# A thresholded attention followed by a SwiGLU block: chunks of 256 tokens instead of 384, two rows of gate or value products per PSUM bank, and an own place for raw weights

## Chip, cores, metric

One core of a Trainium2 chip. Times are device microseconds (us) of one execution; a kernel is timed in several runs, medians are quoted. The rounds ran on different chips, each with the kernel before beside it, so across rounds the ratios to the kernel before are the safer comparison. A profile is one execution recorded by the hardware profiler.

## The reference

```python
# q, k, v: (8 batches, 8 heads, 576 tokens, 64); all fp32
scores = q @ k.T / 8
thresh = max(scores, -1) - 0.02
scores = where(scores >= thresh, scores, -1e9)
attn   = softmax(scores)                       # (+1e-9 in the divisor)
x      = (attn @ v) -> (8*576 tokens, 512)
g      = x @ w_gate                            # w_gate, w_val: 512 x 1536
h      = g * sigmoid(g) * (x @ w_val)
out    = h @ w_out                             # w_out: 1536 x 512
```

## The kernel before

The kernel interleaves two kinds of work. The attention goes in **segments** (a pair of heads), these in **slots** (a tile of 128 queries): segments 0 to 3 have two slots, 4 to 7 three, 8 on five. "Slot 6.1" is slot 1 of segment 6. In each slot the scores, their maximum, the threshold, the exponential and the transposes go through VectorE (DVE), ScalarE (ACT) and GpSimd (POOL), while TensorE (PE) is kept full with **pieces** of the SwiGLU block of an earlier batch: a piece is the gate or value products of a row of 128 hidden units for one chunk of tokens, or three of the twelve accumulating output products (`po`). A slot's share of pieces is its **credit**: what is ready to be done, spread over the slots to come.

The weights arrive as raw 64-bit words in 24 parts. Each part is *fetched* (DMA), *split* on ACT, and *joined* by four DVE and two POOL instructions. A slot joins one. Where a piece asks for a weight that is not there yet, `need` forces further joins in a row, at that place in the program.

```python
    TC = 384                                     # tokens in a chunk
    # raw weights lie in parts of wo not yet filled, and in two buffers of xT
    places += [xp.tile([P, NCC, TC // (2 * G), 2, G], F32, name="xT")... for _ in range(2)]
    # ... (cut)
    def join_weights():
        # ... (cut)
        nc.vector.tensor_scalar(out=up, in0=up, scalar1=1.875 * 2.0 ** -64, ...)             # L169
        nc.vector.tensor_scalar(out=ub, in0=ub, scalar1=3, scalar2=0x7FFFFFFF, ...)          # L171
        nc.vector.scalar_tensor_tensor(out=ub, in0=hi, scalar=0x80000000, in1=ub, ...)       # L173
        nc.vector.tensor_scalar(out=ex.bitcast(U32), in0=ub, scalar1=0xFF800000, ...)        # L175
        nc.gpsimd.tensor_tensor(out=lo, in0=lo, in1=ex, op=ALU.mult)                         # L177
        nc.gpsimd.tensor_tensor(out=up, in0=up, in1=lo, op=ALU.add)                          # L178

    def need(n):                                 # force joins until n parts are there
        while len(joined) < n:
            fetch_weights(2)
            if not split: split_weights()
            join_weights()
            split_weights()

    def gate(j, cs, f, hts, gts):                # value() is alike, its eviction is a multiply on DVE
        # ... (cut)
        need(NCC * (f * P // TC + 1))
        for c in range(NCC):                     # one row: 4 matmuls
            nc.tensor.matmul(ps[:, 0:n], wgv[:, 0, c, f * P:(f + 1) * P], x[:, c, cs], ...)
        nc.scalar.copy(gts[f // per][:, f % per, :], ps[:, 0:n])

    def output(j, rows, hts):
        # ... (cut)
                if f % OF == 0:
                    if any(u[0] == j for u in unsig): sigmoids()
                    need(NCC * DFF // TC + DM // ne * (f * P // TC + 1))
                nc.tensor.matmul(po, hts[f // 2][:, f % 2, i * P:(i + 1) * P], wo[:, f, :], ...)

    # which token ranges are units of work of their own
        if j == 0:   waiting.extend([(0, 0, QA), (0, QA, TC)])        # QA = 256
        elif j == 1: waiting.extend([(1, 0, S - TC), (1, S - TC, TC)])
        else:        waiting.append((j, 0, TC))

    # one slot
            if n or x:
                fetch_weights(2)
                split_weights()
            # ... (cut)
            if more: join_weights()
            fill(part)                           # as many pieces as the credit allows
```

Segments 4 to 7 get the first SwiGLU work: the first 256 tokens of batch 0 are complete then. With chunks of 384 these 256 tokens are a part of chunk 0, whose output products (`wo`, the last weights to arrive) can't be called for before segment 9.

Of the kernel before, what the change touches and what calls it, by code (L numbers as in the profile page):

```python
# [18 lines left out]
def kernel(  # L19
# [42 lines left out]
    TC = 384  # L62
# [5 lines left out]
    assert 2 * D == P and NCC == NP and D == 2 * G and S - SM == 2 * G and 2 * S % TC == 0  # L68
# [6 lines left out]
    xp = ctx.enter_context(tc.tile_pool(name="xp", bufs=4))  # L75
    hp = ctx.enter_context(tc.tile_pool(name="hp", bufs=8))
    gp = ctx.enter_context(tc.tile_pool(name="gp", bufs=4))
    cv = ctx.enter_context(tc.tile_pool(name="cv", bufs=2))
# [19 lines left out]
    for x in sums:  # L98
# [7 lines left out]


# [8 lines left out]
    TW = 2 * TC  # L116
# [3 lines left out]
    places += [xp.tile([P, NCC, TC // (2 * G), 2, G], F32, name="xT").rearrange("p c t a r -> p (c t a r)")  # L120
               for _ in range(2)]
    for f in range(0, DFF, TC):
        for c in range(NCC):
            wpieces.append((wgv[:, :, c, f:f + TC], [w[c * P:(c + 1) * P, f:f + TC] for w in (w_gate, w_val)],
                            len(wpieces) % 4))
    nf, ne = TC // P, TW * P // TC
# [24 lines left out]
    def split_weights():  # L151
        if fetched:
            dst, place = fetched.popleft()
            words = places[place].rearrange("p (m n w) -> p m n w", m=dst.shape[1], w=2)
            lo = cv.tile([P, TW], F32, name="lo").rearrange("p (m n) -> p m n", m=dst.shape[1])
# [266 lines left out]

    unsig = []

    def rows_per(n):

        return 2 * (TC // n)

    def gate(j, cs, f, hts, gts):
# [7 lines left out]
        need(NCC * (f * P // TC + 1))  # L437
        ps = ps_f.tile([P, 512], F32, name="pg", tag="psf")
        x = xts[j].rearrange("p c t a r -> p c (t a r)")
        for c in range(NCC):  # L440
            nc.tensor.matmul(ps[:, 0:n], wgv[:, 0, c, f * P:(f + 1) * P], x[:, c, cs], start=(c == 0), stop=(c == NCC - 1))  # L441
        nc.scalar.copy(gts[f // per][:, f % per, :], ps[:, 0:n])  # L442

    def value(j, cs, f, hts, gts):
        n = cs.stop - cs.start
        per = rows_per(n)
        ps = ps_f.tile([P, 512], F32, name="pv", tag="psf")
        x = xts[j].rearrange("p c t a r -> p c (t a r)")
        for c in range(NCC):
            nc.tensor.matmul(ps[:, 0:n], wgv[:, 1, c, f * P:(f + 1) * P], x[:, c, cs], start=(c == 0), stop=(c == NCC - 1))  # L450
        nc.vector.tensor_tensor(out=hts[f // 2][:, f % 2, cs], in0=gts[f // per][:, f % per, :], in1=ps[:, 0:n],  # L451
                                op=ALU.mult)
        if f % per == per - 1:
            unsig.append((j, gts.pop(f // per), [hts[x][:, :, cs] for x in range((f + 1 - per) // 2, f // 2 + 1)]))
        if f == NF - 1 and cs.stop == TC:
            del xts[j]
# [11 lines left out]
    def output(j, rows, hts):  # L468
        for i in rows:
            po = ps_f.tile([P, 512], F32, name="po", tag="psf")[:, 0:DM]  # L470
            for f in range(NF):
                if f % OF == 0:
                    if any(u[0] == j for u in unsig):
                        sigmoids()
                    need(NCC * DFF // TC + DM // ne * (f * P // TC + 1))
# [16 lines left out]
    for j in range(NCHUNK):  # L492
        if j == 0:
            waiting.extend([(0, 0, QA), (0, QA, TC)])
        elif j == 1:
            waiting.extend([(1, 0, S - TC), (1, S - TC, TC)])
        else:
            waiting.append((j, 0, TC))

    def rows_of(unit):  # L500
        j, lo, hi = unit
        return range(lo // P if j else 0, hi // P if j or hi == TC else 0)
# [13 lines left out]
    def block():  # L516
        late = iter(())
        while True:
# [9 lines left out]
            c = HCOST * (hi - lo) / TC  # L528
            for f in range(NF):
# [22 lines left out]
    def start_batch(b):  # L552
        for j in range(b * S // TC, ((b + 1) * S - 1) // TC + 1):
            if j not in xts:
                while j - 4 in xts:
                    fill(HCOST)
# [82 lines left out]
    for n, seg in enumerate(segs):  # L639
        if NP <= n < 2 * NP:  # L640
            seg["v"] = segs[seg["i"]]["v"]
        for x, t in enumerate(seg["tiles"]):
# [11 lines left out]
            if attends and n > 2 * NP:  # L654
                if prev["i"] % NP == 0:
                    need(NCC * DFF // TC + DM // ne * DFF // TC)
# [4 lines left out]
            if n or x:  # L661
                fetch_weights(2)
                split_weights()
# [16 lines left out]
            if x == len(seg["tiles"]) - 2 and n + 1 < len(segs):  # L680
                prepare(segs[n + 1])
                fetch_qk(segs[n + 1]["i"] + 1)
# [40 lines left out]
```

## Time and profile before

| | before |
|---|---|
| time, median (range) of 3 runs | 1612.72 us (1612.72 to 1615.19) |
| PE busy | 1545.7 us, 96% |
| segments 4 to 7 / segment 8 / segments 9 to 11 | 94.5 / 61.3 / 120.1 us |
| segment 12 starts | 338.2 us |
| segments 12 to 19 / 20 to 34 / 35 to the end | 335.4 / 682.9 / 256.9 us |

Start and length of segments are read off the trace (first score matmul of each). PE is the bound once it is full, from 320 us on. What is to be had lies mostly before that.

### The profile page before, as it was taken

How to read it: one execution, taken by the hardware profiler on the slowest of the kernel's cores; microseconds unless marked ns; L12 is line 12 of the kernel's file. 1: busy time of each engine (PE TensorE's matmuls, PEld its weight loads, DVE VectorE, ACT ScalarE, POOL GpSimd, SP SyncE). 2: the span in 40 equal slices, each digit the busy share in tenths (PEclk: the TensorE clock that was granted, in tenths of full speed). 3: DMA queues.
4: the chain of work that ended last, by engine and by line, in shares of the span. 5: the costliest groups of instructions: out<-in, count | busy, mean ns of one | idle time of the engine just before them, and what ended most of it. 6: DMA issues, size and time to landing. Idle time of an engine off the chain costs nothing.

```text
span 1613.3 us, 28084 instructions
## 1 busy us (share of the span) xinstructions
PE 1545.7 (96%) x10384; PEld 854.9 (53%) x10384; DVE 1082.8 (67%) x3672; ACT 581.2 (36%) x1308; POOL 773.6 (48%) x692
## 2 busy tenths in 40 slices
PE   6899669999999999999999999999999999999998
PEld 4576555558555455455545545455545545455453
DVE  6888868878778778777767768677767767501000
ACT  5777623333333333333323424323323424312011
POOL 3546356554655646646545555636445554402011
PEclk9999889999999999999999999999999999999999
DMA  7442121111111211111011111111011120000000
GB/s 170 131 152 77 56 50 37 44 37 31 31 43 30 50 31 30 43 37 31 7 44 31 30 50 30 43 37 20 13 43 37 30 50 16 8 13 0 13 7 20
DMA packets 176344, 66.70 MB, mean 41 GB/s; under 512 B 159568, under 2 KB 159568, under 8 KB 176208
## 3 DMA queue, kind: packets, MB, share of 16 engines
q1 hardware_dynamic: 173328, 55.47, 15.2%
q0 software_dynamic: 2880, 9.44, 1.5%
q8 instruction: 82, 1.34, 0.3%
q14 instruction: 54, 0.44, 0.1%
HBM read 55.44 MB, written 9.44 MB: 40 GB/s over the span
## 4 chain that ended last, share of the span: by engine, by line
PE 81%; DVE 11%; issue 3%; ACT 3%; POOL 1%; DMA 1%; SPq 1%; DVEq 0%; POOLq 0%; ACTq 0%
PE pg L441 21%; PE pv L450 20%; PE po L476 20%; PE sc L255 9%; PE xa L390 8%; DVE p L295 3%; DVE mx L275 2%; DVE p L321 1%; PE sc L260 1%; ACT p L291 1%; DVE mx L232 1%; PE tp L339 1%; PE xa L362 1%; ACT L291 1%; POOL p L307 1%
## 5 line engine op out<-in xcount | busy, mean ns | idle before, releaser
L307 POOL TENSOR_SCALAR p<-p,ri 128x288 f32<-128x288 f32 x486 | 480.2, 1004 | 432.5 <-DVE ri L303 428.8
L441 PE MATMUL pg<-xT,wgv 128*128 128x384 f32 (+3 forms) x1344 | 410.0, 449 | 15.4 <-ACT gt L442 14.5
L450 PE MATMUL pv<-xT,wgv 128*128 128x384 f32 (+3 forms) x1344 | 407.8, 447 | 9.1 <-ACT gt L442 5.4
L476 PE MATMUL po<-wo,ht 128*128 128x512 f32 x864 | 387.8, 601 | 4.4 <-POOL ht L462 4.4
L441 PEld LDWEIGHTS pg<-xT,wgv 128*128 128x128 f32 x1344 | 243.3, 193 | 162.7 <-issue 24.5
L450 PEld LDWEIGHTS pv<-xT,wgv 128*128 128x128 f32 x1344 | 242.9, 192 | 150.4 <-issue 11.9
L295 DVE SCALAR_TENSOR_TENSOR p<-sc,th,p 128x288 f32<-128x288 f32 (+1 forms) x540 | 258.3, 529 | 47.3 <-ACT p L291 46.5
L476 PEld LDWEIGHTS po<-wo,ht 128*128 128x128 f32 x864 | 160.1, 190 | 210.3 <-issue 194.9
L287 ACT ACTIVATE th<-nm,cut 128x4 f32<-128x4 f32 (+1 forms) x140 | 41.6, 297 | 564.1 <-DVE nm L278 564.1
L275 DVE TENSOR_REDUCE mx<-sc 128x2 f32<-128x576 f32 x252 | 179.6, 750 | 94.7 <-PE sc L255 94.7
L291 ACT ACTIVATE p<-sc,nm 128x288 f32<-128x288 f32 (+1 forms) x540 | 237.1, 511 | 0.6
L451 DVE TENSOR_TENSOR ht<-gt,pv 128x384 f32<-128x384 f32 (+3 forms) x168 | 79.7, 485 | 176.1 <-PE pv L450 170.4
L255 PE MATMUL sc<-kT,qT 64*32 64x288 f32 x4032 | 170.9, 419 | 12.7 <-DVE p L295 12.7
L321 DVE STREAM_TRANSPOSE p<-p 128x576 f32<-128x576 f32 x252 | 181.3, 754 | 0.8 <-POOL p L307 0.8
L462 POOL TENSOR_TENSOR ht<-ht,gt 128x768 f32<-128x768 f32 (+3 forms) x84 | 130.3, 1582 | 95.1 <-ACT gt L460 95.1
L442 ACT COPY gt<-pg 128x384 f32<-128x384 f32 (+3 forms) x168 | 72.5, 439 | 179.1 <-PE pg L441 179.0
L390 PE MATMUL xa<-p,vall 64*64 64x288 f32 x2016 | 129.6, 405 | 0.4 <-issue 0.4
L255 PEld LDWEIGHTS sc<-kT,qT 64*32 64x32 f32 x4032 | 66.6, 107 | 118.1 <-issue 85.9
L390 PEld LDWEIGHTS xa<-p,vall 64*64 64x64 f32 x2016 | 78.2, 133 | 54.2 <-issue 15.4
L207 POOL TENSOR_SCALAR qraw<-qraw,scl 128x576 f32<-128x576 f32 x32 | 55.7, 1742 | 75.8 <-DMA qraw<-in_q_dram 51.8
L232 DVE TENSOR_REDUCE sums<-sums 32x4 f32<-32x4 f32 (+1 forms) x560 | 83.9, 150 | 10.5
L232 DVE TENSOR_REDUCE mx<-mx 32x4 f32<-32x4 f32 (+1 forms) x560 | 83.1, 148 | 10.4
(73 smaller groups left out, 854.4 us busy)
## 6 DMA issues: line engine op xcount, KB each, us to landing
vall<-in_v_dram SPq DMA_DIRECT2D x112, 144.0 KB, 3.5
qraw<-in_q_dram SPq DMA_DIRECT2D x128, 72.0 KB, 2.4
kraw<-in_k_dram SPq DMA_DIRECT2D x128, 72.0 KB, 2.8
out_dram<-ob POOLq DMA_DIRECT2D x36, 256.0 KB, 2.4
wo<-in_moe_w_gate_dram SPq DMA_DIRECT2D x16, 384.0 KB, 3.4
wo<-in_moe_w_val_dram SPq DMA_DIRECT2D x16, 384.0 KB, 4.0
xT<-in_moe_w_out_dram SPq DMA_DIRECT2D x6, 768.0 KB, 5.7
wo<-in_moe_w_out_dram SPq DMA_DIRECT2D x2, 768.0 KB, 4.4
```

The lines of the kernel that those rows point to most:

```text
L232: nc.vector.tensor_reduce(out=x[g * G:(g + 1) * G, 0:m, 1], in_=x[o * G:(o + 1) * G, 0:m, 0:1], axis=AX.X, op=ALU.max)
L255: nc.tensor.matmul(ps[g * G:(g + 1) * G, u, 0:SH], qT[hs, col + a * G:col + (a + 1) * G], kT[hs, c * SH:(c + 1) * SH], start=True, stop=True)
L275: nc.vector.tensor_reduce(out=mx[:, 2 * x:2 * x + 2, 0], in_=tile_[:, :, 0:SH], axis=AX.X, op=ALU.max, negate=True)
L291: nc.scalar.activation(ps[x], scs[x], AF.Exp, bias=nm[:, x:x + 1])
L295: nc.vector.scalar_tensor_tensor(out=ps[x], in0=scs[x], scalar=th[:, x:x + 1], in1=ps[x], op0=ALU.is_ge, op1=ALU.mult, accum_out=sm[:, x, ...
L307: nc.gpsimd.tensor_scalar(out=ps[x], in0=ps[x], scalar1=ri[:, x:x + 1], scalar2=None, op0=ALU.mult)
L321: nc.vector.transpose(out=p, in_=p)
L390: nc.tensor.matmul(xa[a][h * D:(h + 1) * D, at:at + n * G].rearrange("d (i q) -> d i q", q=G), vr[rs, h, j, :], p[rs, lo:lo + n, j, :], st ...
L441: nc.tensor.matmul(ps[:, 0:n], wgv[:, 0, c, f * P:(f + 1) * P], x[:, c, cs], start=(c == 0), stop=(c == NCC - 1))
L450: nc.tensor.matmul(ps[:, 0:n], wgv[:, 1, c, f * P:(f + 1) * P], x[:, c, cs], start=(c == 0), stop=(c == NCC - 1))
L462: nc.gpsimd.tensor_tensor(out=ht, in0=ht, in1=gt[:, 2 * x:2 * x + 2, :], op=ALU.mult)
L476: nc.tensor.matmul(po, hts[f // 2][:, f % 2, i * P:(i + 1) * P], wo[:, f, :], start=(f == 0), stop=(f == NF - 1))
```

## The change

Intent: one chunk of 256 fills half a PSUM bank, so two rows share a bank and an eviction takes both (114 evictions for each matrix instead of 168); the first 256 tokens are a whole chunk; raw weights get a place of their own and are loaded a slot ahead of their split, so that no split waits for a load.

```diff
-    TC = 384
+    TC = 256
+    FW = 384                                   # width of a part of the weights, as before
+    spare = const.tile([P, 6 * TW], F32, name="spare")
-    places += [xp.tile(... name="xT") ... for _ in range(2)]
+    places += [spare[:, n * 2 * TW:(n + 1) * 2 * TW] for n in range(2)]
+    los = deque(spare[:, n * TW:(n + 1) * TW] for n in (4, 5))
 ... (cut)
+    GR = 2
+    def rows_of_products(j, cs, f, mat, name):  # 2 rows, 8 matmuls, one bank
+        for i in range(GR):
+            for c in range(NCC):
+                nc.tensor.matmul(ps[:, i], wgv[:, mat, c, (f + i) * P:(f + i + 1) * P], x[:, c, cs], ...)
-        need(NCC * (f * P // TC + 1))
+        need(NCC * ((f + GR - 1) * P // FW + 1))
 ... (cut)
+        ends = [lo for lo in (QA - j * TC, S - j * TC) if 0 < lo < TC]     # cuts chunk 2 at 64
+        waiting.extend((j, lo, hi) for lo, hi in zip([0, *ends], [*ends, TC]))
-        return range(lo // P if j else 0, hi // P if j or hi == TC else 0)
+        return range(TC // P if hi == TC else 0)
 ... (cut)
-                    need(NCC * DFF // TC + DM // ne * DFF // TC)    # all weights, at segment 9
             if n or x:
+                split_weights()
                 fetch_weights(2)
-                split_weights()
+            if x == 0 and n >= NP:
+                fetch_qk(seg["i"] + 1)          # q and k at a segment's start, no longer at its end
```

The parts cut here also give the transposed tokens (`xT`) six buffers for four and the gates (`gt`) five for four.

More of the change, by code (lines that the diff above doesn't have):

```diff
@@ L61 @@
     SH = S // 2
-    TC = 384
+    TC = 256
+    XB = 6
     NCHUNK = B * S // TC
@@ L67 @@
     SCALE = 1.0 / float(D) ** 0.5
-    assert 2 * D == P and NCC == NP and D == 2 * G and S - SM == 2 * G and 2 * S % TC == 0
+    assert 2 * D == P and NCC == NP and D == 2 * G and S - SM == 2 * G and B * S % TC == 0
     const = ctx.enter_context(tc.tile_pool(name="const", bufs=1))
@@ L74 @@
     stp = ctx.enter_context(tc.tile_pool(name="stp", bufs=4))
-    xp = ctx.enter_context(tc.tile_pool(name="xp", bufs=4))
+    xp = ctx.enter_context(tc.tile_pool(name="xp", bufs=XB))
     hp = ctx.enter_context(tc.tile_pool(name="hp", bufs=8))
-    gp = ctx.enter_context(tc.tile_pool(name="gp", bufs=4))
-    cv = ctx.enter_context(tc.tile_pool(name="cv", bufs=2))
+    gp = ctx.enter_context(tc.tile_pool(name="gp", bufs=5))
     op = ctx.enter_context(tc.tile_pool(name="op", bufs=1))
@@ L105 @@
     wo = const.tile([P, NF, DM], F32, name="wo")
-    TW = 2 * TC
+    FW = 384
+    TW = 2 * FW
+    spare = const.tile([P, 6 * TW], F32, name="spare")
     wpieces = deque()
@@ L119 @@
     places = [land[:, n * 2 * TW:(n + 1) * 2 * TW] for n in range(NF * DM // (2 * TW))]
-    places += [xp.tile([P, NCC, TC // (2 * G), 2, G], F32, name="xT").rearrange("p c t a r -> p (c t a r)")
-               for _ in range(2)]
-    for f in range(0, DFF, TC):
+    places += [spare[:, n * 2 * TW:(n + 1) * 2 * TW] for n in range(2)]
+    los = deque(spare[:, n * TW:(n + 1) * TW] for n in (4, 5))
+    for f in range(0, DFF, FW):
         for c in range(NCC):
-            wpieces.append((wgv[:, :, c, f:f + TC], [w[c * P:(c + 1) * P, f:f + TC] for w in (w_gate, w_val)],
+            wpieces.append((wgv[:, :, c, f:f + FW], [w[c * P:(c + 1) * P, f:f + FW] for w in (w_gate, w_val)],
                             len(wpieces) % 4))
-    nf, ne = TC // P, TW * P // TC
+    nf, ne = FW // P, TW * P // FW
     wplaces = deque([4, 5, 2, 3] + [4, 5] * 2)
@@ L154, in split_weights @@
             words = places[place].rearrange("p (m n w) -> p m n w", m=dst.shape[1], w=2)
-            lo = cv.tile([P, TW], F32, name="lo").rearrange("p (m n) -> p m n", m=dst.shape[1])
+            lo = los[0].rearrange("p (m n) -> p m n", m=dst.shape[1])
+            los.rotate(1)
             nc.scalar.activation(dst, words[:, :, :, 1], AF.Abs, scale=2.0 ** -80)
@@ L425, in rows_per @@
     def rows_per(n):
-        return 2 * (TC // n)
+        return 2 if n > P else 4
+    GR = 2
+    def rows_of_products(j, cs, f, mat, name):
+        n = cs.stop - cs.start
+        ps = ps_f.tile([P, 512], F32, name=name, tag="psf")[:, 0:GR * n].rearrange("p (f n) -> p f n", n=n)
+        x = xts[j].rearrange("p c t a r -> p c (t a r)")
+        for i in range(GR):
+            for c in range(NCC):
+                nc.tensor.matmul(ps[:, i], wgv[:, mat, c, (f + i) * P:(f + i + 1) * P], x[:, c, cs],
+                                 start=(c == 0), stop=(c == NCC - 1))
+        return ps
     def gate(j, cs, f, hts, gts):
@@ L436, in gate @@
             gts[f // per] = gt[:, 0:per * n].rearrange("p (f n) -> p f n", n=n)
-        need(NCC * (f * P // TC + 1))
-        ps = ps_f.tile([P, 512], F32, name="pg", tag="psf")
-        x = xts[j].rearrange("p c t a r -> p c (t a r)")
-        for c in range(NCC):
-            nc.tensor.matmul(ps[:, 0:n], wgv[:, 0, c, f * P:(f + 1) * P], x[:, c, cs], start=(c == 0), stop=(c == NCC - 1))
-        nc.scalar.copy(gts[f // per][:, f % per, :], ps[:, 0:n])
+        need(NCC * ((f + GR - 1) * P // FW + 1))
+        ps = rows_of_products(j, cs, f, 0, "pg")
+        nc.scalar.copy(gts[f // per][:, f % per:f % per + GR, :], ps)
     def value(j, cs, f, hts, gts):
@@ L446, in value @@
         per = rows_per(n)
-        ps = ps_f.tile([P, 512], F32, name="pv", tag="psf")
-        x = xts[j].rearrange("p c t a r -> p c (t a r)")
-        for c in range(NCC):
-            nc.tensor.matmul(ps[:, 0:n], wgv[:, 1, c, f * P:(f + 1) * P], x[:, c, cs], start=(c == 0), stop=(c == NCC - 1))
-        nc.vector.tensor_tensor(out=hts[f // 2][:, f % 2, cs], in0=gts[f // per][:, f % per, :], in1=ps[:, 0:n],
+        ps = rows_of_products(j, cs, f, 1, "pv")
+        nc.vector.tensor_tensor(out=hts[f // 2][:, :, cs], in0=gts[f // per][:, f % per:f % per + GR, :], in1=ps,
                                 op=ALU.mult)
-        if f % per == per - 1:
-            unsig.append((j, gts.pop(f // per), [hts[x][:, :, cs] for x in range((f + 1 - per) // 2, f // 2 + 1)]))
-        if f == NF - 1 and cs.stop == TC:
+        if f % per == per - GR:
+            unsig.append((j, gts.pop(f // per), [hts[x][:, :, cs] for x in range((f + GR - per) // 2, f // 2 + 1)]))
+        if f == NF - GR and cs.stop == TC:
             del xts[j]
@@ L474, in output @@
                         sigmoids()
-                    need(NCC * DFF // TC + DM // ne * (f * P // TC + 1))
+                    need(NCC * DFF // FW + DM // ne * (f * P // FW + 1))
                 nc.tensor.matmul(po, hts[f // 2][:, f % 2, i * P:(i + 1) * P], wo[:, f, :],
@@ L492 @@
     for j in range(NCHUNK):
-        if j == 0:
-            waiting.extend([(0, 0, QA), (0, QA, TC)])
-        elif j == 1:
-            waiting.extend([(1, 0, S - TC), (1, S - TC, TC)])
-        else:
-            waiting.append((j, 0, TC))
+        ends = [lo for lo in (QA - j * TC, S - j * TC) if 0 < lo < TC]
+        waiting.extend((j, lo, hi) for lo, hi in zip([0, *ends], [*ends, TC]))
     def rows_of(unit):
         j, lo, hi = unit
-        return range(lo // P if j else 0, hi // P if j or hi == TC else 0)
+        return range(TC // P if hi == TC else 0)
     def cost(unit):
@@ L527, in block @@
             hts, gts = hidden.setdefault(j, {}), {}
-            c = HCOST * (hi - lo) / TC
-            for f in range(NF):
+            c = GR * HCOST * (hi - lo) / TC
+            for f in range(0, NF, GR):
                 if f == (EARLY if j else 0):
@@ L554, in start_batch @@
             if j not in xts:
-                while j - 4 in xts:
+                while j - XB in xts:
                     fill(HCOST)
@@ L681 @@
                 prepare(segs[n + 1])
-                fetch_qk(segs[n + 1]["i"] + 1)
+                if n < NP:
+                    fetch_qk(segs[n + 1]["i"] + 1)
         prev = seg
```

## The prediction

> **What bounds the kernel now.** I read the page first (parts 1, 2, 4), then the chain in order of time, then a table by stretches, then the timelines of the stretches where the matmul engine (PE) idles.
>
> ```profile
> span 1613.3 us, 28084 instructions
> PE 1545.7 (96%) x10384; PEld 854.9 (53%) x10384; DVE 1082.8 (67%) x3672; ACT 581.2 (36%) x1308; POOL 773.6 (48%) x692
> PE   6899669999999999999999999999999999999998
> DVE  6888868878778778777767768677767767501000
> PEclk9999889999999999999999999999999999999999
> ...
> PE 81%; DVE 11%; issue 3%; ACT 3%; POOL 1%; DMA 1%; SPq 1%; DVEq 0%; POOLq 0%; ACTq 0%
> ```
>
> PE is full from slice 8 on (40 us a slice): its idle time, 1613 - 1546 = 67 us, and its slow clock lie almost all in the first 320 us. Is a full PE at its best rate? The chain shows groups of eight gate or value records; each fp32 matmul leaves two records.
>
> ```profile
> 89.32 1.73 PE pv L450 x8
> 234.20 1.30 PE pv L450 x8
> 419.29 2.58 PE pv L450 x8
> ```
>
> These are widths 256, 192 and 384: 216, 162 and 322 ns a record, 0.84 ns a column in all three. So from slice 8 on only less PE work would help. The early part, with cuts at starts of scores:
>
> ```profile
> core 0: us, PE busy (x) PEld busy (x) DVE busy (x) ACT busy (x) POOL busy (x), PEclk, DMA share, GB/s
> 72.17:156.76 84.59, 82.80 (x579) 59.60 (x577) 71.56 (x151) 64.85 (x123) 44.24 (x26) 1.00 0.32 99
> 156.76:218.03 61.27, 38.71 (x354) 29.70 (x353) 49.73 (x143) 31.77 (x69) 28.36 (x17) 0.79 0.34 85
> 218.03:261.05 43.02, 39.12 (x355) 27.04 (x355) 34.02 (x117) 15.26 (x38) 20.01 (x19) 0.94 0.04 8
> 261.05:298.18 37.13, 35.36 (x272) 16.93 (x271) 31.61 (x118) 11.35 (x32) 26.11 (x29) 1.00 0.20 47
> ```
>
> The kernel runs in segments (a pair of heads each; 0 to 3 of two slots, 4 to 7 of three, 8 on of five). Segments 4 to 7 (62 to 157 us) have PE full. Segment 8 takes 61 us and has PE idle for 22; segment 9 takes 43; segment 10, with no weight work left, 37 at 85% DVE: that is the DVE-bound floor. In segments 8 and 9 the weights' joins (four DVE, two POOL operations a piece) are in the way, and one stall:
>
> ```profile
> 208.26 0.56 SPq L145 DMA_DIRECT2D xT<-in_moe_w_out_dram  x1
> 214.13 0.90 ACT L156 ACTIVATE wo<-xT 128x768 f32<-128x768 f32 x1 [7.97 <-DMA xT<-in_moe_w_out_dram]
> 216.02 2.08 PE L441 MATMUL pg<-xT,wgv 128*128 128x128 f32 x8 [9.42 <-ACT gt L442]
> ```
>
> The last weight load is issued in the slot that splits it, behind eight q/k loads that wait for DVE; ACT waits 8 us for it, PE 9.4 us for ACT. This the change removes.
>
> **What the Trainium skill says.** "TensorE: Matmul & The Clock Gate", section "Back-to-back issue gap", gives an isolated gap of N / 2.4 + 2.5 ns. The trace agrees with a pass of 2N columns per record: 384 gives 322.5, measured 322. So narrower chunks cost about 2.5 ns a record, little. The same page, section "Part 1: The HAM clock gate", says idle PE falls back to half clock; the trace has 0.79 in 157 to 218 us. "ScalarE: Activation LUTs", section "What ACT_TABLE_LOAD costs", gives about 1283 ns a load plus a drain; the trace has 1283 for each of 44. "PSUM — Partial Sum Buffer", section "The four PSUM rules": an output fits one bank of 512 fp32, so two rows of 256 fill one; the trace can't test it beyond the 512-wide output products.
>
> **The change, part by part.**
> (a) PE work. Gate and value have 1344 records each: 960 of 384 columns, 192 of 192, 96 of 256, 96 of 128. After: 19 units of 48 matmuls, 1824 records each: 1632 of 256, 96 of 192, 96 of 64. Old: 960 x 0.3225 + 192 x 0.1625 + 96 x 0.216 + 96 x 0.11 = 372 us. New: 1632 x 0.216 + 96 x 0.1625 + 96 x 0.08 (my estimate) = 376 us. Both matrices: +8 us, of which some +4 fall in the PE-bound part.
> (b) Evictions. 168 copies (72.5 us on ACT) become 114. By slope over the widths 256 and 384 (413, 541 ns on DVE), 512 takes about 670 ns on DVE; a 512 copy on ACT has 590 already. DVE saves some 6 us, ACT 8; in segments 8 to 11, DVE-bound, perhaps 5.
> (c) Sigmoids. They run once three units of two rows wait. Such units are a third smaller, so table pairs rise from 22 to about 33: +28 us on ACT, at 36% busy, hidden.
> (d) Loads. Splitting before fetching, own places, and q/k loads at a segment's start take away the 8 us stall and, in part, POOL's 52 us of waits on q. The latter lie beside a full PE: nothing.
> (e) Order of FFN work, the part that the few words do not name. I counted by hand from the code's credit rule which pieces fall in which slot. Chunk 0 is now complete with 256 tokens, so its output products belong to segments 4 to 8, and the pace rises. Before: 21 pieces of 1.73 us in segments 4 to 7, 36 us; after: 12 pieces of 3.45 and 3 output pieces of 2.57, 49 us. PE is full there: +13 us. The weights are wanted earlier, too: a pair of rows asks for the column block of its second row, and output weights are asked for at segment 7 instead of 9. Joins still go one a slot, else they are forced in a row. What one takes:
>
> ```profile
> 76.20 1.25 PE L260 MATMUL sc<-p 64*128 64x288 f32 x8
> ...
> 81.17 0.54 DVE L169 TENSOR_SCALAR wgv<-wgv 128x768 f32<-128x768 f32 x1
> ...
> 83.40 0.56 DVE L175 TENSOR_SCALAR wo<-wgv 128x768 uint32<-128x768 uint32 x1
> ...
> 84.09 1.82 POOL L177 TENSOR_TENSOR lo<-lo,wo 128x768 f32<-128x768 f32 x1 [3.08 <-ACT p L309]
> ...
> 86.00 1.82 POOL L178 TENSOR_TENSOR wgv<-wgv,lo 128x768 f32<-128x768 f32 x1
> ```
>
> The slot starts at 76.2, DVE joins at +5 to +7.8, POOL ends at +11.6. PE reaches its product at +3 to +5. Each further join in the slot adds about 3.7 us on POOL. Slots that now need a piece joined in the same slot, by my count: 4.1 (piece 7: wait about 5.5 us), 5.2 (piece 11: 5.7), 6.1 (pieces 13 to 15 in a row: POOL ends near +19, wait about 14), 7.2 (pieces 19 to 21: about 11), and 8.0 (22 and 23: the slot takes about 20). PE is in order, so the next scores stand behind the product and DVE idles meanwhile.
> Sum: segments 4 to 7 took 94.5 us; +13 work +36 waits, less some 6 already idle there: about 137. Segment 8: 20 + 26 (four slots at the floor) = 46 for 61. Segments 9 to 11: 37 each, 111 for 120. Net 43 - 15 - 9 = +19; less (b) 5 = +14; plus (a) 4 = +18; less about 4 for small waits that go (a tail with a smaller last chunk, q waits). About +13: 1612.7 + 13 = 1626 us.
>
> **The rivals.**
> R1, gain: the early stall goes, forced joins hide. DVE and POOL are at 85% and 52% in 72 to 157 us, so joins could overlap with pieces PE still has. Then segments 4 to 7 cost only the 13 us of work and segments 8 to 11 win 24: 1613 - 24 + 13 - 5 + 4 = about 1600. For it: the only join wait on PE before is 0.3 us. Against it: PE is in order and the product that waits is next in its queue.
> R2, nothing: PE is full at its best rate from 350 us on, all work moved is the same work, gains and losses early cancel: 1610 to 1617.
> R3, a new wait in the steady part: pieces of 3.45 us instead of 2.58 are coarser, and sigmoids forced just before an output product make PE wait for POOL (4.4 us in 3 times before). If each of some 30 rounds cost 1 us: 1645 to 1655. Against it: my count gives two forced rounds, for three before; slots with two pieces now hold 6.9 us, better matched to the DVE chain of 6.5 us a slot.
>
> **Range and chances.** My sum stands on waits estimated by hand; half of them gone gives 1608, R1 1600; all of them plus a cold clock after each (a restart record group took 2.08 instead of 1.06 us) gives some 1645. 8 in 10: 1600 to 1648. Faster by 2% (under 1580.5) would need 32 of the early idle us back with nothing paid: 0.05. Slower by 2% (over 1645): 0.12. Within 2%: 0.83.
>
> **What would show it.** Right: eight gate records of 256 in 1.73 us; segments 4 to 7 longer than 94.5 us with PE waits of 5 to 15 us on POOL's join in slots 6.1, 7.2, 8.0; no wait on the last weight load; segments 9 to 11 near 37 us; table loads near 66; the distance from segment 12 to the end the same within 6 us. Wrong: no PE waits on joins (then R1), or a steady part that is longer (R3), or a record of 256 that takes more than 0.22 us once streams are long.

## The result, and the profile after

| | before | after |
|---|---|---|
| time, median (range) | 1613.91 us (1612.72 to 1615.19) | 1702.55 us (1701.63 to 1704.14) |
| ratio, 95% interval | | 1.055 (1.0532 to 1.0568), slower |
| segments 4 to 7 | 94.5 us | 161.9 us |
| segment 8 | 61.3 | 54.1 |
| segments 9 to 11 | 120.1 | 121.2 |
| segment 12 starts | 338.2 | 398.7 (+60.5) |
| segments 12 to 19 | 335.4 | 351.8 (+16.4) |
| segments 20 to 34 | 682.9 | 683.2 (+0.3) |
| 35 to the end | 256.9 | 266.2 (+9.3) |

First the page of the kernel after, parts 1, 2 and 4 (40 slices of 42.5 us):

```profile
span 1699.9 us, 30018 instructions
PE 1569.8 (92%) x11344; PEld 1040.5 (61%) x11344; DVE 1094.6 (64%) x3642; ACT 603.0 (35%) x1315; POOL 797.0 (47%) x740
...
PE   6876648889999999999999999999999999899998
...
PEclk9987869899999999999999999999999999999999
...
PE 73%; DVE 9%; issue 3%; POOL 3%; ACT 2%; POOLq 0%; DVEq 0%; ACTq 0%
```

Counted from 0, PE was at 9 tenths in slices 2 and 3 before, and at 6 in the two after them; now it is at 4 to 7 from slice 2 to slice 5, and its clock falls to 6 tenths in slice 5. In the chain POOL has 3% for 1%. The table by stretches shows the same for segments 4 to 7 and segment 8 (columns as in the prediction's table). Segments 4 to 7 before:

```profile
62.26:156.76 94.50, 91.07 (x637) 65.26 (x637) 76.77 (x162) 73.24 (x139) 49.12 (x29) 0.98 0.34 105
```

Segments 4 to 7 and segment 8 after (segment 8 before is in the prediction):

```profile
61.50:223.40 161.90, 114.01 (x678) 76.37 (x679) 102.90 (x176) 85.25 (x148) 71.28 (x41) 0.84 0.26 81
223.40:277.50 54.10, 32.08 (x256) 16.90 (x255) 35.30 (x108) 12.25 (x30) 26.73 (x23) 0.81 0.11 27
```

In segments 4 to 7 of the kernel after no engine is full: PE 70%, DVE 64%, POOL 44%. The engines wait for one another, one after the other. The waits of PE name the place. Kernel before (engine, line, waited for: total us, times, longest):

```profile
PE pg L441 <- ACT gt L442: 14.5, 2, 9.4
PE sc L255 <- DVE p L295: 12.7, 20, 1.9
```

Kernel after:

```profile
PE po L485 <- POOL wo L181: 38.7, 4, 19.8
PE sc L258 <- DVE p L298: 29.1, 29, 3.9
PE pg L440 <- POOL wgv L181: 27.6, 5, 8.2
...
PE xa L393 <- DVE p L324: 6.0, 1, 6.0
```

PE's stall of 9.4 us is gone. In its place PE waits 66.3 us for the last instruction of forced joins (L181), nine times: 46.4 us of it in segments 4 to 7 and 19.8 in slot 8.0. It waits 16.4 us more than before for the scores' buffers (L298), nearly all from segment 9 on. ACT's own wait on a weight load, which the change was to remove, is still there, before and after:

```profile
ACT wo L156 <- DMA xT<-in_moe_w_out_dram: 8.0, 1, 8.0
ACT wo L159 <- DMA spare<-in_moe_w_out_dram: 7.4, 1, 7.4
```

In slot 7.2 two loads are issued at 210.36 us, and the first of them is split at 214.77. PE does not wait for this split: at that time it waits for an earlier join. The timeline of slot 6.1 shows a row of joins (start, duration, in brackets the idle time before it and its releaser). The first two lines are the lone join of slot 6.0, for comparison:

```profile
138.04 0.56 DVE L174 TENSOR_SCALAR wgv<-wgv 128x768 uint32<-128x768 uint32 x1
138.64 0.96 DVE L176 SCALAR_TENSOR_TENSOR wgv<-wo,wgv 128x768 uint32<-128x768 uint32 x1
...
147.47 1.99 POOL L180 TENSOR_TENSOR spare<-spare,wo 128x768 f32<-128x768 f32 x1 [3.36 <-ACT wgv L159]
147.84 2.04 DVE L174 TENSOR_SCALAR wgv<-wgv 128x768 uint32<-128x768 uint32 x1
149.54 2.00 POOL L181 TENSOR_TENSOR wgv<-wgv,spare 128x768 f32<-128x768 f32 x1
149.91 2.44 DVE L176 SCALAR_TENSOR_TENSOR wgv<-wo,wgv 128x768 uint32<-128x768 uint32 x1
151.57 0.91 ACT L160 ACTIVATE spare<-wo 128x768 f32<-128x768 uint32 x1 [4.65 <-POOL wgv L181]
...
151.59 1.22 PE L440 MATMUL pg<-xT,wgv 128*128 128x256 f32 x2 [5.64 <-POOL wgv L181]
...
157.26 1.22 PE L440 MATMUL pg<-xT,wgv 128*128 128x256 f32 x2 [4.45 <-POOL wgv L181]
...
162.50 1.22 PE L440 MATMUL pg<-xT,wgv 128*128 128x256 f32 x2 [4.02 <-POOL wgv L181]
```

A lone join has its two middle DVE instructions in 0.56 and 0.96 us. In the row they take 2.04 and 2.44 us, because they run beside POOL's two instructions of the join before (e6 tests this). Each starts while one of these runs and ends 0.42 and 0.81 us after the end of that one (149.46 and 151.54). Further joins therefore end 5.7 and 5.2 us apart (PE's starts at 151.59, 157.26 and 162.50), and not 3.7 us; in slot 7.2 5.8 and 5.7 us, and in slot 8.0, where POOL also has 4.64 us of p's normalisation (L310) to do between two joins, 8.3 us. ACT's half of a split also waits for POOL to free its buffer (4.65 us). Each further join releases one matmul (two records) of the second row of the pair, and PE stands again.

Where streams are long, the records have the predicted rate: within a group they start 216 ns apart. 16 records of 256 columns, two rows, take from start to start 480.13 - 476.58 = 3.55 us with the change of work, 222 ns each:

```profile
476.58 3.62 PE L440 MATMUL pg<-xT,wgv 128*128 128x256 f32 x16
```

### The profile page after: what moved, and what is told of

It is laid out like the page before. It is cut to its first block, busy times and chain, and to the rows that moved or that the text cites. A ratio compares the mean times of both kernels' runs of the same rounds, so it can differ in the third digit from the quotient of the medians.

```text
span 1699.9 us, 30018 instructions
## 1 busy us (share of the span) xinstructions
PE 1569.8 (92%) x11344; PEld 1040.5 (61%) x11344; DVE 1094.6 (64%) x3642; ACT 603.0 (35%) x1315; POOL 797.0 (47%) x740
## 4 chain that ended last, share of the span: by engine, by line
PE 73%; DVE 9%; issue 3%; POOL 3%; ACT 2%; POOLq 0%; DVEq 0%; ACTq 0%
PE po L485 19%; PE pg L440 19%; PE pv L440 19%; PE sc L258 8%; PE xa L393 8%; DVE p L298 2%; DVE mx L278 2%; POOL p L310 2%; DVE p L324 1%; DVE mx L235 1%; ACT L294 1%; ACT p L294 1%; POOL ht L471 1%; DVE sums L235 0%; POOL wo L181 0%
## 5 line engine op out<-in xcount | busy, mean ns | idle before, releaser
L310 POOL TENSOR_SCALAR p<-p,ri 128x288 f32<-128x288 f32 x504 | 498.0, 1004 | 515.0 <-DVE ri L306 513.1
L440 PE MATMUL pg<-xT,wgv 128*128 128x256 f32 (+2 forms) x1824 | 408.1, 377 | 27.6 <-POOL wgv L181 27.6
L440 PE MATMUL pv<-xT,wgv 128*128 128x256 f32 (+2 forms) x1824 | 406.0, 376 | 0.0
L440 PEld LDWEIGHTS pg<-xT,wgv 128*128 128x128 f32 x1824 | 335.7, 192 | 96.5 <-POOL wgv L181 30.2
L440 PEld LDWEIGHTS pv<-xT,wgv 128*128 128x128 f32 x1824 | 335.3, 191 | 65.3 <-issue 14.6
L298 DVE SCALAR_TENSOR_TENSOR p<-sc,th,p 128x288 f32<-128x288 f32 (+1 forms) x540 | 258.5, 529 | 57.4 <-ACT p L294 56.8
L460 DVE TENSOR_TENSOR ht<-gt,pv 128x512 f32<-128x512 f32 (+2 forms) x114 | 73.6, 645 | 209.7 <-PE pv L440 205.8
L471 POOL TENSOR_TENSOR ht<-ht,gt 128x512 f32<-128x512 f32 (+2 forms) x114 | 135.5, 1216 | 82.8 <-ACT gt L469 82.8
L454 ACT COPY gt<-pg 128x512 f32<-128x512 f32 (+2 forms) x114 | 64.4, 566 | 179.9 <-PE pg L440 173.9
L490 POOL DMA_DIRECT2D out_dram<-ob x36 | 21.5, 599 | 165.8 <-ACT ob L489 165.8
L408 DVE COPY xT<-xa 128x128 f32<-128x128 f32 (+3 forms) x80 | 17.8, 249 | 114.7 <-PE xa L393 106.7
```

What stands on the lines that cost most here:

```text
L298: nc.vector.scalar_tensor_tensor(out=ps[x], in0=scs[x], scalar=th[:, x:x + 1], in1=ps[x], op0=ALU.is_ge, op1=ALU.mult, accum_out=sm[:, x, ...
L310: nc.gpsimd.tensor_scalar(out=ps[x], in0=ps[x], scalar1=ri[:, x:x + 1], scalar2=None, op0=ALU.mult)
L440: nc.tensor.matmul(ps[:, i], wgv[:, mat, c, (f + i) * P:(f + i + 1) * P], x[:, c, cs], start=(c == 0), stop=(c == NCC - 1))
L460: nc.vector.tensor_tensor(out=hts[f // 2][:, :, cs], in0=gts[f // per][:, f % per:f % per + GR, :], in1=ps, op=ALU.mult)
L471: nc.gpsimd.tensor_tensor(out=ht, in0=ht, in1=gt[:, 2 * x:2 * x + 2, :], op=ALU.mult)
```

## The experiments

The theory after the first look: (T1) chunk 0's output products, which now count in the credit from segment 4 on and are called for from slot 7.1 on, force joins in a row; these make nearly all of it. Rivals: (T2) the new order of loads or the own places cost; (T3) contention of DVE and POOL makes the row slow; (T4) coarse pieces, two rows at a time, cost PE in the steady part; (T5) the narrow products of chunk 2, cut at 64, cost. Twelve kernels were run. Ratios are against the kernel before in the same rounds; a verdict of faster or slower would need 2%, so several smaller differences below are "same" by that rule although their interval leaves out 1.

**e1: hold chunk 0's output products until segment 8.** Only the output products move, and their credit with them (to chunk 1); all else is the kernel after.

```diff
-                yield from late
+                if not held[0]:
+                    yield from late
+            if n == 2 * NP and x == 1:
+                held[0] = False
-        return 2 * NF * HCOST * ... + len(rows_of(unit)) * NF / OF * OCOST
+        return 2 * NF * HCOST * ... + {0: 0, 1: 2}.get(unit[0], 1) * len(rows_of(unit)) * NF / OF * OCOST
```

> The changed kernel with one thing undone: the output products of chunk 0 are held back until segment 8, as they came before the change, so the pace in segments 4 to 7 falls to its old value and, by my count of the pieces, no join of weights is forced in a row (before this edit: three forced rows, in slots 6.1, 7.2 and 8.0). Theory J (the early demand for joined weights cost the time): PE's waits on POOL's join fall from 66 us to under 10, segments 4 to 7 from 162 us to 95-105, segment 12 starts near 335-345 us instead of 399, and the time is 1625-1640 us. Rival W (narrower, coarser products cost the time everywhere): above 1680 us. Rival L (the new order of the loads cost it): above 1680 us.

Measured: 1652.41 us, ratio 1.0243 (1.0224 to 1.0261), correct. 50 us of the 89 come back, so T1 is the largest part, but the time is 12 us above the range expected. Segments 4 to 7 take 98.2 us (after 161.9, before 94.5). Two waits on joins are left, 18.4 us where under 10 were expected, in slots 9.1 and 7.0:

```profile
PE po L485 <- POOL wo L181: 12.8, 1, 12.8
...
PE pg L440 <- POOL wgv L181: 5.6, 1, 5.6
```

**e2: the kernel before with the new order of loads alone.** Split ahead of fetch, and q and k at a segment's start. (The own place for raw weights was not tried there: by my count, which no run checks, the kernel before is some 6.7 KB per partition short of memory for it.)

```diff
+                split_weights()
                 fetch_weights(2)
-                split_weights()
+            if x == 0 and n >= NP:
+                fetch_qk(seg["i"] + 1)
```

> The kernel before with only the load part of the change that fits its memory: split ahead of fetch, and the q/k loads at a segment's start instead of behind the transposes; chunks of 384, weights' places as before. Theory J: this part is a gain of its own, the 8 us wait of ACT on the last weight load goes, segment 8 shrinks from 61 to about 50 us, and the time is 1600-1610 us against 1613. Rival L: 1640 us or more, segments 4 to 8 longer.

Measured: 1603.43 us, ratio 0.9934 (0.9911 to 0.9956), correct. This part is a gain of 10 us, and T2 falls for the order of loads. Segment 8 takes 52.8 us for 61.3, segment 12 starts at 326.3 us for 338.2. It is the fastest correct kernel of the study.

**e3 and e4: no joins at all, in the kernel after and in the kernel before.** Wrong results on purpose: the six instructions of a join are left out, everything else, `need` too, stays.

```diff
-        nc.vector.tensor_scalar(out=up, in0=up, scalar1=1.875 * 2.0 ** -64, ...)
-        ... (the four DVE and two POOL instructions of a join)
         joined.append(up)
```

> Wrong result on purpose: the changed kernel without the six operations of each join (four on DVE, two on POOL); loads, splits and the order of everything else stay. Theory J: PE's 66 us of waits on the join go, and segments 4 to 8 shrink from 216 us to 130-150; the time is 1590-1620 us, and its distance to the kernel before under the same cut (next run) falls from 89 us to 15-30, the rest being the 64-wide products, the last attention product, which waits 6 us, and 4 us of records. Rival W or L: the distance stays at 60 us or more.

> Wrong result on purpose: the kernel before without the six operations of each join. It is the base for the run above. Theory J: joins are little on its path outside segments 8 and 9, so 1575-1600 us against 1613: segment 8 at 40-50 us instead of 61, segment 9 at 37-40. Rivals: no different number here; they differ by the distance of the two.

Measured: after 1624.35 us (ratio 1.0065, 1.005 to 1.008), before 1590.93 us (ratio 0.9861, 0.9844 to 0.9878). The joins cost the kernel before 23 us and the kernel after 78 us. Without them the distance is 33 us, not 89: some 55 us of the distance are joins, and 33 us are something else. Of the 35 us between the two profiled spans, 7.6 us lie before segment 12, 17.8 us in segments 12 to 19 and 9.4 us from segment 35 on. So T1 alone does not settle the case. Two expectations missed: the distance was to be 15 to 30 us, and segment 8 of e4 40 to 50 us (54.9).

e3 also separates two things in segments 4 to 7. It has the same pieces there as the kernel after (678 matmul records in both). Without joins PE is busy 104.5 us with them at a granted clock of 0.97, with joins 114.0 us at 0.84. So the waits cost PE some 9.5 us a second time, by the lower clock.

**e5: e1, and chunk 2 not cut at the end of batch 0.** No unit of 64 or 192 columns is left; 1728 records for each matrix instead of 1824.

```diff
-        ends = [lo for lo in (QA - j * TC, S - j * TC) if 0 < lo < TC]
+        ends = []
```

> The held version of the changed kernel (1652 us), with chunk 2 no longer cut at the end of batch 0: no product of 64 or 192 columns is left. In the changed kernel's trace the 64-wide records start 113 to 131 ns apart, where 64 columns at 0.84 ns would be 54, so 192 of them cost some 23 us for 10 us of columns. Theory N (a record of 64 columns is bound by something other than its columns, and this is part of what is left of the loss): 12 us less PE work, part of it where PE is not full; time 1640-1648 us, segments 8 to 11 shorter by 5 us or more. Rival (harmless there, and 64 tokens now come later, into the part where PE is full): 1652-1660 us.

Measured: 1633.01 us, ratio 1.0123 (1.0108 to 1.0138), correct. 19 us less than e1, more than expected. 17.4 of them lie in segments 8 to 11 (167.8 us for 185.2), where PE is busy 141.3 us instead of 150.4, and where the wait of 12.8 us on the last output weights is down to 4.4 us; 3.2 in segments 12 to 19. So T5 holds. In the kernel after 16 records of 64 columns take 1.78 us at full clock (the lines are under e7), 111 ns each; at 0.84 ns a column they would take 54. The cut thus costs 96 x 111 + 96 x 162 ns for each matrix instead of 96 x 216: 5.5 us, 11 us for both. In segments 8 to 11 the gain is accounted for: 9.1 us less PE work and 8.4 us less of that one wait. Why the wait shrinks with the cut gone was not tested.

**e6: the kernel after, with the joins' two POOL instructions on DVE.** Not timed in rounds.

```diff
-        nc.gpsimd.tensor_tensor(out=lo, in0=lo, in1=ex, op=ALU.mult)
-        nc.gpsimd.tensor_tensor(out=up, in0=up, in1=lo, op=ALU.add)
+        nc.vector.tensor_tensor(out=lo, in0=lo, in1=ex, op=ALU.mult)
+        nc.vector.tensor_tensor(out=up, in0=up, in1=lo, op=ALU.add)
```

> The changed kernel with the two POOL operations of each join moved to DVE. In the changed kernel's forced rows of joins the DVE operations of the second and third join take 2.0 and 2.4 us, where the same ones take 0.56 and 0.96 in a lone join, and each ends just after POOL's multiply or add that runs beside it. Theory C (DVE and POOL hold each other up when both run): without POOL in the join, all 24 of the shift operations take under 0.8 us and all 24 of the sign operations under 1.2, though the joins still come in a row. Rival S (they wait for ACT's split or for a buffer): some still take 2 us. Time 1685-1715 us, since DVE gets 24 x 1.9 us more and the row of three still ends about 20 us after the slot's start.

Measured: 1705.16 us, correct. The instruction at line 174 by itself, in e6 (minimum/median/maximum in ns):

```profile
L174 DVE TENSOR_SCALAR wgv<-wgv x16: 559/560/561, 28.0 to 166.0; 128x768 uint32<-128x768 uint32 x16
```

Its longest is 561 ns, where the kernel after has 2041 ns. So POOL's instructions do slow DVE's, and T3 is shown as a fact. The other eight at this line (into `wo`) take at most 693 ns, for 1911. One bound of the expectation was missed: at line 176 two of 24 take 1.38 us, for 1.2 expected; both run beside POOL's scaling of q (L210), which was left on POOL.

What the contention costs in time e6 does not say, for it has a price of its own: one join now has six DVE instructions one after the other, 0.60 + 0.70 + 0.97 + 0.96 + 0.97 + 0.96 = 5.2 us in the chain. The equal total hides two effects. Where joins are not forced, this costs: segment 4 starts at 71.6 us for 61.5. Where they are, it gains 7.0 us: segments 4 to 7 take 159.7 us (161.9), segment 8 49.3 (54.1); slots 6.1, 7.2 and 8.0 take 27.8, 30.9 and 23.5 us (28.6, 32.2 and 28.3). Further joins in slot 6.1 end 4.7 us apart, in slots 7.2 and 8.0 5.4 us. A row of joins is thus long either way, on POOL and DVE with contention or on DVE alone without.

The Trainium skill, "GPSIMD Engine Reference", section "Specifications", says that the engine's SBUF interfaces are shared with VectorE, with contention for DVE instructions in a 2-port perf mode or with two SBUF inputs. The trace agrees for line 176 with two inputs, which goes from 0.96 to 2.44 us beside POOL. Line 174 with one goes from 0.56 to 2.04 us; whether it runs in such a mode no run here shows.

**e7: the kernel after, with one row a bank.**

```diff
-    GR = 2
+    GR = 1
-        nc.vector.tensor_tensor(out=hts[f // 2][:, :, cs], ...)
+        nc.vector.tensor_tensor(out=hts[f // 2][:, f % 2:f % 2 + GR, cs], ...)
```

> The changed kernel with one row per PSUM bank instead of two; chunks of 256 and all else stay. 228 evictions of 256 columns instead of 114 of 512: +6 us on DVE, +8 on ACT, pieces of 1.73 us. Theory J: the two rows are not what costs, 1690-1710 us; forced rows of joins stay in slots 6.1, 7.2 and 8.0. Rival P (coarse pieces of 3.45 us make the loss): 1660 us or less.

Measured: 1679.10 us, ratio 1.0417 (1.0394 to 1.044), correct. The expectation missed: two rows a bank cost 23 us, although e7 has twice the evictions for each unit. And e7 even lost some 12 us in one place (an estimate: half of the 24 us from 391.7 to 416 us). In slot 12.1 its 64-wide records ran at half clock. The timeline of e7, and its stretch (length, PE busy, ..., granted clock third from the end):

```profile
401.63 1.91 PE L440 MATMUL pg<-xT,wgv 128*128 128x64 f32 x8
403.34 1.91 PE L440 MATMUL pv<-xT,wgv 128*128 128x64 f32 x8
...
394.70:416.00 21.30, 21.00 (x105) 20.64 (x99) 6.65 (x27) 3.02 (x11) 6.94 (x8) 0.50 0.00 0
```

Eight records take 1.71 us there. In the kernel after, 16 take 413.12 - 411.34 = 1.78 us at full clock:

```profile
411.34 1.95 PE L440 MATMUL pg<-xT,wgv 128*128 128x64 f32 x16
```

**e8: the kernel after, with the old order of loads.** The reverse of e2.

```diff
-                split_weights()
                 fetch_weights(2)
+                split_weights()
-            if x == 0 and n >= NP:
-                fetch_qk(seg["i"] + 1)
```

> The changed kernel with the order of the loads of before: fetch ahead of split, q/k loads behind the transposes. The same step taken on the kernel before gave 1614 to 1603 us. Theory J: the order is a gain here too, or lost behind the forced joins: 1700-1715 us. Rival L (the new order costs): under 1690 us.

Measured: 1700.60 us, ratio 1.0542 (1.0527 to 1.0558), correct. The order makes no difference here: 2 us. POOL's waits on q rise from 11.8 to 41.5 us, and that costs nothing. My reading was that the forced joins, which set segments 4 to 8, hide what e2 gained. e12 shows another reason to be possible: there the order makes no difference without forced joins.

**e9: e5, and one row a bank.** Left of the change: the chunk width, the own place, the order of loads.

```diff
-    GR = 2
+    GR = 1
```

> The kernel of e5 (chunk 0's output products held, chunk 2 not cut) and in it one row of gate or value products a bank again, as in e7. What is left of the change is then the chunk width of 256, the own place for raw weights and the earlier loads. Theory (the rest of e5's distance is the coarse pieces of two rows a bank: e7 was 23 us faster than after with that part alone undone): 1605 to 1620 us, segments 12 to 19 below 345 us (e5 352.2, before 335.4) and no stretch at half clock, as no 64-wide products are left. Rival (what e7 saved was time beside the forced joins, 13 us of it in segments 4 to 7, which e5 no longer has): 1626 to 1635 us.

Measured: 1613.29 us, ratio 0.9999 (0.9982 to 1.0017), correct. 20 us less than e5, and nothing is left of the distance. T4 is shown. The ratio of 1.000 is a sum of two parts that cancel. Segment 12 starts at 326.6 us, as early as in e2 (326.3; before 338.2). From there on e9 takes 9.9 us more than the kernel before (1285.0 us for 1275.1), and PE is busy 10.9 us more (1271.35 for 1260.44): that is what the narrower chunks and the own place leave. Part (a) of the prediction had some +4 for it, with the cut. Of e5's and e9's difference, 12.3 us lie in segments 12 to 19 and 6 us from segment 35 on. Segments 12 to 19 of e5 (table of stretches, waits of PE):

```profile
328.10:680.20 352.10, 338.48 (x2677) 218.73 (x2676) 265.44 (x963) 127.74 (x296) 191.41 (x186) 0.99 0.17 36
...
PE sc L258 <- DVE p L298: 9.2, 11, 1.9
PE po L485 <- POOL ht L471: 4.4, 2, 2.2
```

The same of e9:

```profile
326.60:666.40 339.80, 334.98 (x2678) 217.23 (x2677) 265.22 (x977) 128.69 (x319) 189.56 (x183) 0.99 0.16 36
...
PE po L485 <- POOL ht L471: 2.7, 2, 2.2
PE sc L258 <- DVE p L298: 2.1, 2, 1.9
```

The same matmuls to one (2677 and 2678), the same work of DVE. With pieces of 16 records (3.55 us) PE stands 9.2 us for scores' buffers, in 11 places; with pieces of eight, 2.1 us in two. The waits, the 1.7 us less on POOL's `ht` among them, make 8.8 of the 12.3 us, PE's busy time the other 3.5.

**e10: e9, and three output products ahead of the last attention product.** In after, e1 and e5 that product waits 6 us for its transposed probabilities, with nothing left to fill.

```diff
         prev = seg
+    fill(3 * OCOST)
     turn(0)
```

> The kernel of e9, and three output products more are called for ahead of the last attention product, which in after, e1 and e5 waits some 6 us for its transposed probabilities with no filling product left. Theory (that wait is on the path): 3 to 6 us below e9 where e9 shows the wait, and the same as e9 where it does not (e7, with one row a bank, showed none): in all 1600 to 1618 us. Rival: the three products are only moved, what ends last is the train of output products, no change to e9 within 0.2%.

Measured: 1608.47 us, ratio 0.9972 (0.9956 to 0.9988), correct: 4.8 us below e9, 4.3 of it from segment 35 on (256.5 us for 260.8). In e9 the profile had put 2.4 us there down to "issue", not to a wait on data, so the gain is somewhat more than the idle time that I could name.

**e11: the kernel after with the edit of e10 alone.**

> The kernel after, with the three output products ahead of the last attention product as the only edit. Theory: the wait of 6.04 us there goes or shrinks below 2.5 us, 1695 to 1700 us against 1702.6. Rival (there is nothing else left to do then, so the products that fill it are missing elsewhere): 1702 to 1704 us.

Measured: 1695.09 us, ratio 1.0507 (1.049 to 1.0523), correct. The wait is gone, segment 35 to the end takes 259.1 us for 266.2. So filling this wait of 6 us brings back 7 of the 9.3 us that the change loses at the end.

**e12: e9 with the old order of loads.** Left of the change: the chunk width and the own place.

```diff
-                split_weights()
                 fetch_weights(2)
+                split_weights()
-            if x == 0 and n >= NP:
-                fetch_qk(seg["i"] + 1)
```

> The kernel of e9 with the order of loads of the kernel before: fetch ahead of split, and q and k only after the slots. What is then left of the change is the chunk width of 256 with its own place for raw weights. Theory (without forced joins the order is worth what e2 showed it worth in the kernel before, 10 us, and the narrower products cost about as much): 1620 to 1627 us, segment 8 some 8 us longer than e9's 45.8. Rival (the own place for raw weights alone already takes the waits of segment 8 away): 1611 to 1616 us, segment 8 within 2 us of e9's.

Measured: 1614.50 us, ratio 1.001 (0.9993 to 1.0027), correct. The theory put down there falls, its rival holds: segment 8 takes 46.5 us (e9 45.8). With an own place for raw weights the order no longer matters; where the place is shared, as in the kernel before, it is worth 10 us (e2). That a load then waits for no other user of the buffer is the likely reason, argued and not tested by itself.

The ladder from after down, each step on top of the one above it; the last row stands by itself. The steps in us cross rounds and chips, the ratios do not:

| kernel | us | ratio | step |
|---|---|---|---|
| after | 1702.55 | 1.0550 | |
| e1: chunk 0's outputs held | 1652.41 | 1.0243 | -50 |
| e5: and chunk 2 not cut | 1633.01 | 1.0123 | -19 |
| e9: and one row a bank | 1613.29 | 0.9999 | -20 |
| e10: and the last wait filled | 1608.47 | 0.9972 | -5 |
| e2: before, with the new order of loads alone | 1603.43 | 0.9934 | |

The steps depend on their order; e7 shows that one row a bank alone saves 23 us in the kernel after, 14 of it before segment 12, beside the forced joins.

## Why the prediction was wrong

The direction (slower) and the first mechanism were right: chunk 0's output products force joins, and PE waits for POOL's last instruction of a join in slots 4.1, 5.2, 6.1, 7.2 and 8.0, all of them named (only 1.1 us in slot 7.1 was not). The count of pieces was right, too: 12 gate or value pieces (of 16 records) and 3 output pieces in segments 4 to 7. The size was off: +13 us predicted, +89 measured, outside the range. By the terms of its sum:

| term | predicted | measured |
|---|---|---|
| segments 4 to 7 | 137 us | 161.9 us |
| of which: more work for PE | +13 | +13.5 (by e3, at clock 0.97) |
| of which: a lower clock | 0 | +9.5 (0.84 for 0.97) |
| of which: PE's waits on joins | +36 | +46.4 |
| of which: other idle time that goes | -6 | -1.9 |
| segment 8 | 46 | 54.1 |
| segments 9 to 11 | 111, less 5 | 121.2 |
| from segment 12 on, added | +4, less some for a tail with a smaller last chunk | +26.0 |

The two spans differ by 86.6 us, 73 more than the sum: 24 of them lie in segments 4 to 7, 8 in segment 8, 15 in segments 9 to 11 and 26 from segment 12 on. The steps that failed:

1. **"Each further join in the slot adds about 3.7 us on POOL."** The step took POOL's two instructions of 1.82 us as the bound and let DVE's four run beside them at the durations of a lone join. In the row they contend, and a further join takes 5.2 to 5.8 us, 8.3 in slot 8.0. In slot 6.1 the last join ends 22.9 us after the slot's start, for "+19". That its waits sum to 14.1 us, for "about 14", is luck: PE had some records to do in between. In slot 7.2 the first join already ends at +15.2, for +11.6, since the chain runs through two table loads of 1.28 us, sigmoids and the normalisation of p before its first DVE instruction; the waits are 17.7 us, for "about 11". Slot 8.0 takes 28.3 us, for "about 20", and this is all that segment 8 is too long. I had counted the joins by their number, not what else is queued ahead of them on three engines. e6, without contention, has rows nearly as long with six instructions in a row on DVE, so it does not tell how much of these sizes is contention and how much the queue.
2. **The clock after each wait** had no term in the sum, only the upper end of the range ("a cold clock after each"). It was 0.84 in segments 4 to 7 and 0.81 in segment 8, and cost 9.5 us in the former.
3. **Rival R3, coarse pieces, was set aside wrongly.** "Slots with two pieces now hold 6.9 us, better matched to the DVE chain of 6.5 us a slot" was an argument by averages. PE runs its matmuls in the order of the program, so a piece of 3.55 us can delay the next scores by up to that much when the scores' buffers come free in the middle of one. This reading fits the waits (9.2 us in 11 places for 2.1 in two), but no run tests it apart from the number of rows. e9 against e5 measures 20 us for the two rows, 12.3 of them in segments 12 to 19. My own test, "the distance from segment 12 to the end the same within 6 us", fails with 26 us. But in segments 20 to 34 nothing is lost (+0.3 us): there PE is full either way.
4. **The 64-wide products.** Part (a) estimated 80 ns a record, "96 of 64"; they take 111 ns. That is 192 x 31 ns = 6 us. The larger loss was not in the estimate at all: e5 gains 19 us without the cut, 8.4 of them in one wait on the last output weights.
5. **The tail.** "A tail with a smaller last chunk" was to gain a few us. It lost 9.3: the filling pieces run out ahead of the last attention product, which then waits 6 us (e11: 7 us back). That wider steps of credit are why they run out was not tested.
6. **Segments 9 to 11, "37 each"**, took 35.6, 43.6 and 42.0 us; segment 11 took 40.0 before. With one row a bank (e7) or without joins (e3) they stay at 121 us, so neither alone is the reason, and it stays open.
7. **"No wait on the last weight load"** came true for PE only. ACT still waits 7.4 us for one, for 8.0 before, for a load issued 4 us earlier. In e1, e2 and e9 this wait is gone. What it was worth was judged well: e2 gains 8.5 us in segment 8.
8. **Right as predicted:** 216 ns for a 256-wide record in a group; 512-wide evictions of 674 ns on DVE (670 predicted) and 589 ns on ACT; 31 and 30 table loads for 33 pairs; POOL's waits on q down from 51.8 to 11.8 us, worth nothing (e8).
9. **Rival R1** ("forced joins hide") falls with the first waits of PE; R2, gains and losses that cancel, would have been right for the change without its three costly parts: e9 and e12 stand at 1.000 and 1.001.

What stays open: why the wait on the last output weights shrinks in e5, why segments 9 to 11 did not fall to 111 us, what contention alone costs, and why the clock fell to half in e7's slot 12.1 and not in the same slot of the kernel after.

## What to carry to other kernels

When work is made available earlier, ask first what data it needs and when that is ready: an engine that works in program order and meets an early product stands for everything that is queued behind it, and a preparation that is cheap at one a slot (24 joins cost the kernel before 23 us) costs its full length, and more, when it is forced in a row (78 us in the kernel after). A larger piece of filling work saves evictions on engines that have time and costs the engine that has none its flexibility; here two rows a bank cost 20 us, and the evictions that they saved gained nothing that e7 or e9 shows. Check such an argument by undoing the parts one at a time: the best kernel here (e2) is the kernel before with the one small reordering of the change, a few lines of it. And read a zero by stages: e6 against after and e9 against before look like no effect and are each two effects that cancel.

## What the Trainium skill lacked or had wrong

- "TensorE: Matmul & The Clock Gate", section "LDWEIGHTS (loading the stationary operand)", gives P / 1.2 ns for loading P columns. My estimate worked out from it is 107 ns for 128 columns, near the 111 ns from one 64-wide record to the next here, while the estimate from columns alone (80) was too low. The load records themselves last 192 ns each and overlap, and no run tests that loading sets the pace.
- The same page, section "Part 1: The HAM clock gate", gives half clock as the state after an idle window of about 3.4 us, and warns that the gate has also been seen stuck low. e7 adds a case without such a window: the clock fell at some 391.7 us, no idle time of PE in the 30 us before was longer than 1.93 us, and it stayed at 0.50 with PE 99% busy in the 21.3 us from 394.7 on. The kernel after ran the same products at full clock. Why in one and not in the other, no run here settles.
- No page tells of the cost of coarse filling pieces on PE: 20 us of 1613 for groups of 16 records instead of eight (e5 against e9).
